# Retention followed by a two-layer dense block on one core: token order restored in the copy ahead of the dense product, stores of whole rows, casts of v behind the copies of k and q, and block 1 computed undivided

## The chip, the cores and the metric

The kernel runs on one core of a Trainium2 chip. A core has five engines that each work through their own list of instructions in order: TensorE (PE, matrix products; its weight loads are listed apart as PEld), VectorE (DVE), ScalarE (ACT), GpSimd (POOL) and SyncE (SP, which here only issues DMAs). Waiting is done on semaphores, and 16 DMA engines move data between the main memory and the core's SBUF. TensorE writes to PSUM, eight banks of 128 partitions by 512 fp32; VectorE and ScalarE read it. The metric is the device time of one execution in microseconds; lower is better.

## The reference

Four batches of eight heads, 768 tokens each, head width 64: for each head, a state of 64 x 64 decays by a factor gamma per token and takes in k v^T, and each token's output is q times the state. The eight heads of a token side by side make a row of 512, and 3072 such rows go through a dense block with a leaky activation:

```python
for t in range(S):
    state = gamma * state + k[t] v[t]^T          # per batch and head
    y[t]  = scale * q[t] state
x = y.transpose(0, 2, 1, 3).reshape(3072, 512)   # heads side by side
h = x @ w_in                                     # 512 x 2048
g = max(h, 0) + alpha * min(h, 0)
out = g @ w_out                                  # 2048 x 512, rows in token order
```

## The kernel before, in words

**Windows and blocks.** The recurrence is computed in chunks. A window `w` is 256 tokens of one batch and four heads (group g of two); there are 24. Four windows (512 tokens, both groups) make a block `n` of the dense part; there are six. A chunk c is half a window, 128 tokens. In SBUF a partition p holds the token pair 2p, 2p+1 (the loads at L141 read "h (p a) d -> p h (a d)"), so the tokens of a chunk are kept as a parity a and an index i: column 64a + i.

**A window's steps.** `load` (L135) issues three DMAs for k, q and v on SP. `prep` (L150) scales k and q into `kdq` (L158, on POOL or DVE) and casts v to fp16 into `vx` (L176 on ACT for windows 0 to 7, L178 on POOL later). k and q must be transposed into `kq`: windows 0 to 7 do it in `turn` (L189) with eight TensorE transposes into a PSUM tile `trb` and one ACT copy (L201); windows 8 to 23 do it with a transposing DMA that SP issues (L171). `scores` (L214) makes 16 small products into the PSUM tile `sc`; `state_sums` (L238) sums k v^T into `st`; `masked` (L254, DVE) applies the mask to `sc`; `state` (L265, DVE) updates the state `tg`; `within` (L299) makes the outputs `y` from the carried state (L286) and from the products within the chunk (L308), then sets a small DVE memset (L317) that tells they are through; `finish` (L321) adds the other carried products and copies `y` from PSUM to SBUF as fp16, `xT` (L329, ACT). `y` and `sc` have one buffer each, so `within` of a window waits for the copy of the window before it. `visit(old, new)` is the usual order: `within(old)`, `scores(new)`, `state_sums(new)`, `finish(old)`, `masked(new)`, `state(new)`.

**Token order before.** `xT` keeps the columns parity by parity, so the dense product's row 64a + i of 128 rows is token 2i + a, and the store (L435) puts them back on the way out: `out[row : row + 128, :].rearrange("(p a) m -> a p m", a=2)`.

**Dense part.** `ffn1` (L370) computes 16 tiles of 128 x 512, each with four matmuls (L377, moving operand `xT[n][:, hp, :]`, 512 columns); ACT takes relu of minus the tile (L367) and DVE combines (L356) into `gt`. `ffn2` (L412) has four groups of 16 matmuls (L422), each closed by an ACT copy (L431) and a store of 256 KB (L435). Both are generators that are advanced matmul by matmul with `tick(gen, m)`: the order is written out by hand, and each engine runs its instructions in that order. Block 1's first product runs as two halves of 256 columns (`ffn1_half`, L388, matmuls at L398), between which windows 6 and 7 are worked in (L540 to L564).

**The opening** (L446 to L514): windows 0 to 3 one after another, with filler matmuls (`busy`, L181) that write an unused tile. The weights come by eight DMAs issued on POOL (`get_wi`, `get_wo`); the loads of windows 4 to 11 wait for the third `get_wo`.

**The later blocks** (L566 on): `ahead` (L551) puts `prep(w)` and the loads of window w+4 in between; SP thus issues, in program order, transposing DMAs, loads and stores from one queue.

Of the kernel before, what the change touches and what calls it, by code (L numbers as in the profile page):

```python
# [10 lines left out]
F16 = mybir.dt.float16  # L11
# [7 lines left out]
def kernel(  # L19
# [15 lines left out]
    nc = tc.nc  # L35
# [7 lines left out]
    WB = 4  # L43
# [106 lines left out]
    def prep(w, opening=False, k_on=None):  # L150
        u, g, b, c3 = place(w)
        t = staged.pop(w)
        kdq = sbp.tile([128, 2, 4, 2, D], F16, tag="kdq", bufs=8, name=f"kdq{w}")
        vx = sbp.tile([128, 4, 2, D], F16, tag="vx", bufs=8, name=f"vx{w}")
        kq = sbp.tile([128, 8, 128], F16, tag="kq", bufs=8, name=f"kq{w}")

        def scaled(eng, kind, src):
            eng.tensor_tensor(  # L158
                out=kdq[:, kind].rearrange("p z r d -> p r z d"),
                in0=src.rearrange("p (r x) (a d) -> p r (x a) d", a=2, x=2),  # L160
                in1=tab[:, 16 * kind + 8 * g : 16 * kind + 8 * g + 8]
                .rearrange("p (r z) -> p r z", r=2)
                .unsqueeze(3)
                .to_broadcast([128, 2, 4, D]),
                op=MULT,
            )

        scaled(k_on or (nc.vector if opening else nc.gpsimd), 0, t["k"])
        scaled(nc.gpsimd, 1, t["q"])
        if w >= NPE:  # L170
            nc.sync.dma_start_transpose(  # L171
                out=kq, in_=kdq.rearrange("p k z r d -> p (k z r d)")
            )
        v_in = t["v"].rearrange("p h (a d) -> p h a d", a=2)
        if opening:
            nc.scalar.activation(out=vx, in_=v_in, func=COPY, bias=0.0, scale=1.0)  # L176
        else:
            nc.gpsimd.tensor_copy(out=vx, in_=v_in)  # L178
        prepped[w] = (kdq, kq, vx)

    def busy(m):  # L181

# [3 lines left out]
                out=ips[:, 0:128], lhsT=ones, rhs=ones, start=True, stop=True  # L186
            )

    def turn(w, tag, fill=0):  # L189
        kdq, kq, vx = prepped[w]  # L190
        flat = kdq.rearrange("p k z r d -> p (k z r d)")
        trb = ps("trb", tag, 1024, F16)
        for i in range(8):
            if i == 4 and fill:
                busy(fill)
            nc.tensor.transpose(  # L196
                out=trb[:, 128 * i : 128 * i + 128],
                in_=flat[:, 128 * i : 128 * i + 128],
                identity=ident,
            )  # L200
        nc.scalar.activation(  # L201
            out=kq.rearrange("p b i -> p (b i)"),
            in_=trb[:, 0:1024],
            func=COPY,
            bias=0.0,
            scale=1.0,
        )

    DIAG = [(0, 0), (1, 1), (0, 1), (1, 0)]

# [67 lines left out]
    def carried(w, y, started, same, after=None):  # L278
        u, g, b, c3 = place(w)
        kq = live[w][1]  # L280
        for x in range(2):
            for r in range(2):
                c = r if same else 1 - r
                if c3 + c == 0:
                    continue
                ins = nc.tensor.matmul(  # L286
                    out=y[half(x), 512 * c + 128 * r : 512 * c + 128 * r + 128],
                    lhsT=tgs[2 * u + c, g][half(r), x, :],
                    rhs=kq[half(r), 4 + 2 * x : 6 + 2 * x, half(c)],
                    start=(c, x) not in started,  # L290
                    stop=not same,
                    skip_group_check=True,
                )
                started.add((c, x))
                if after is not None:
                    behind(ins, after, "the other row half wrote this bank")
                    after = None

    def within(w):  # L299
        u, g, b, c3 = place(w)  # L300
        vx, m2 = live[w][2:4]
        y = ps("y", "y", 1024, FP, 1)
        started = set()
        carried(w, y, started, True)
        for r in range(2):
            for a in range(2):
                for c, x in DIAG:
                    last = nc.tensor.matmul(  # L308
                        out=y[half(x), 512 * c + 128 * r : 512 * c + 128 * r + 128],
                        lhsT=vx[half(c), 2 * r + x, a, :],  # L310
                        rhs=m2[half(c), 2 * r + x, a, :],
                        start=(c, x) not in started,
                        stop=(a == 1 and (c == r or c3 + c == 0)),
                        skip_group_check=True,
                    )
                    started.add((c, x))
        done = nc.vector.memset(warm[0:1], 0.0)  # L317
        behind(done, last, "tells that the products within the chunks are through")
        live[w].append((y, started, done))

    def finish(w):  # L321
# [3 lines left out]
        live.pop(w)  # L325
        n, i = divmod(u, 2)
        if w % WB == 0:
            xT[n] = sbp.tile([128, NP, TB], F16, tag="xT", bufs=2, name=f"xT{n}")
        nc.scalar.activation(  # L329
            out=xT[n][:, 2 * g : 2 * g + 2, TU * i : TU * i + TU].rearrange(  # L330
                "p r (c i) -> p c r i", c=2
            ),
            in_=y.rearrange("p (c z) -> p c z", c=2)[:, :, 0:256].rearrange(
                "p c (r i) -> p c r i", r=2
            ),
            func=COPY,
            bias=0.0,
            scale=1.0,
# [31 lines left out]
    def ffn1(n, order="spyfSpYf"):  # L370
# [3 lines left out]
        for ft in range(NFT):  # L374
            hps = banks.next("hps")
            for hp in range(NP):
                nc.tensor.matmul(  # L377
                    out=hps,
                    lhsT=w_in_all[:, hp, 128 * ft : 128 * ft + 128],
                    rhs=xT[n][:, hp, :],  # L380
                    start=(hp == 0),
                    stop=(hp == NP - 1),
                )
                if hp == NP - 1:
                    prelu(gt, ft, hps, 0, TB, minus(hps))
                yield

    def ffn1_half(n, i, order):  # L388
        if i == 0:
            gts[n] = sbp.tile([128, NFT, TB], F16, tag="gt", bufs=2, name=f"gt{n}")  # L390
        gt = gts[n]
        lo, hi = TU * i, TU * i + TU
        banks = Banks(order)
        for f0 in range(0, NFT, 2):
            hps = banks.next("hps")
            for j in range(2):
                for hp in range(NP):
                    nc.tensor.matmul(  # L398
                        out=hps[:, TU * j : TU * j + TU],
                        lhsT=w_in_all[:, hp, 128 * (f0 + j) : 128 * (f0 + j) + 128],  # L400
                        rhs=xT[n][:, hp, lo:hi],
                        start=(hp == 0),
                        stop=(hp == NP - 1),
                    )
                    if j == 1 and hp == NP - 1:
                        hm = minus(hps)
                        for z in range(2):
                            s = slice(TU * z, TU * z + TU)
                            prelu(gt, f0 + z, hps[:, s], lo, hi, hm[:, s])
                    yield  # L410

    def ffn2(n, parts=1, order="f"):  # L412
        gt = gts.pop(n)
# [3 lines left out]
        for f0 in range(0, NFT, step):  # L417
            for tq in range(4):
                if f0 == 0:
                    opss[tq] = banks.next("ops")  # L420
                for ft in range(f0, f0 + step):
# [7 lines left out]
                    if ft == NFT - 1:  # L429
# [2 lines left out]
                            out=os_sb, in_=opss[tq], func=COPY, bias=0.0, scale=1.0  # L432
                        )
                        row = TB * n + 128 * tq
                        nc.sync.dma_start(  # L435
                            out=out[row : row + 128, :].rearrange("(p a) m -> a p m", a=2),
                            in_=os_sb,
                        )
                    yield

    def tick(gen, m):
# [32 lines left out]
    aps = ps("aps", "f")  # L474
    nc.tensor.transpose(out=aps[:, 0:NFT], in_=alpha_sb, identity=tab[0:NFT, ALT : ALT + NFT])
    prep(2, opening=True)
    get_wi(0)
    state(0)
    nc.vector.tensor_scalar(
        out=oma_sb, in0=aps[:, 0:NFT], scalar1=-1.0, scalar2=1.0, op0=MULT, op1=ADD  # L480
    )
    turn(1, "f")
    within(0)
    scores(1)
    state_sums(1)
    finish(0)
    masked(1)
    prep(3, opening=True, k_on=nc.gpsimd)
    state(1)
    turn(2, "f")  # L490
    within(1)
    scores(2)
    state_sums(2, (0,))
    finish(1)
    masked(2)
    state(2, (0,))
    turn(3, "f")
    within(2)
    scores(3)
    state_sums(3, (0,))  # L500
    finish(2)
    masked(3)
    state(3, (0,))
    for i in range(1, 4):
        get_wi(i)
    get_wo(0)
    get_wo(1)
    held.append(get_wo(2))
    get_wo(3)
    within(3)  # L510
    busy(8)
    finish(3)
    for w in range(WB, 3 * WB):
        load(w)  # L514

    gen = ffn1(0)
    tick(gen, 32)
    for w in (2, 3):
        state_sums(w, (1,))
        state(w, (1,))  # L520
    for _ in gen:
        pass
    gen = ffn2(0)
    for w in range(WB, 2 * WB):
        prep(w, opening=True)
    tick(gen, 30)
    turn(4, "p")
    tick(gen, 6)
    visit(None, 4)
    tick(gen, 7)  # L530
    turn(5, "p")
    tick(gen, 6)
    visit(4, 5)
    tick(gen, 7)
    turn(6, "p")
    tick(gen, 6)
    visit(5, 6)
    for _ in gen:
        pass
    gen = ffn1_half(1, 0, "ffpp")  # L540
    tick(gen, 8)
    turn(7, "f")
    tick(gen, 8)
    visit(6, 7)
    tick(gen, 16)
    visit(7, None)
    for _ in gen:
        pass
    more = [8]

    def ahead():  # L551
# [4 lines left out]
                load(w + WB)  # L556
            more[0] += 1

    gen = ffn1_half(1, 1, "spyfSpYf")
    for i in range(WB):  # L560
        tick(gen, 14)
        ahead()
    for _ in gen:
        pass  # L564

    for n in range(1, NBLK):  # L566
        if n > 1:
            gen = ffn1(n)
            for i in range(2):
                tick(gen, 20)  # L570
                ahead()
            for _ in gen:
                pass
        gen = ffn2(n)
        if n + 1 < NBLK:
            w0 = WB * (n + 1)
# [46 lines left out]
```

## Time and profile before

| what | value |
|---|---|
| median of three runs | 246.69 us (243.04 to 247.25) |
| the profiled execution's own time | 245.44 us |
| its span, first to last instruction | 243.6 us |
| around the span | 1.84 us |
| PE busy | 212.6 us, 87% of the span |
| DVE, ACT, POOL busy | 130.5, 99.3, 58.4 us |
| granted TensorE clock, mean | 0.925 of full |
| moved by DMA | 34.08 MB |

A profile is read from its stages: for each stretch of the span, which engine is busy throughout, and where TensorE stands idle, what it waited for. A window of the trace gives the busy time of each engine in that stretch, the granted clock, the mean share of the 16 DMA engines that was busy, and GB/s. Shares over 1 occur, since a packet's time is counted where it ends. A matmul's listed duration contains its pipeline's length; the chain of work that ended last shows the spacing instead.

### The profile page before, as it was taken

The numbers are of one execution on the slowest core, as the hardware profiler recorded it, in microseconds if no ns is written. First come the engines' busy times: TensorE is split into PE (matmuls) and PEld (weight loads), VectorE is DVE, ScalarE is ACT, GpSimd is POOL, SyncE is SP. The second block draws the span as 40 slices with busy tenths as digits, with TensorE's granted clock in tenths as the row PEclk, the third lists the DMA queues.
The fourth block names the chain that finished last, engine by engine and source line by source line (L and its number), as shares of the span: only waits on it lengthen the run. The fifth ranks groups of instructions, "written<-read, shape, count | busy, mean of one in ns | idle before, by whom it ended". The sixth has DMA issues, their size and how long they took to land.

```text
span 243.6 us, 5296 instructions
## 1 busy us (share of the span) xinstructions
PE 212.6 (87%) x2215; PEld 112.3 (46%) x2215; DVE 130.5 (54%) x242; ACT 99.3 (41%) x162; POOL 58.4 (24%) x69
## 2 busy tenths in 40 slices
PE   8557999999489999999989999599999999999500
PEld 8445444456358654444444445244445444444200
DVE  1535288635639964288644786142887526840000
ACT  2353366454436423465114663024663126631100
POOL 1591002596000654410243501262000000000000
PEclk9955599999979999999999999979999999999955
DMA  7999998993195999695999699695993111001110
GB/s 209 317 169 205 201 211 256 311 340 109 51 71 136 237 230 153 176 74 167 96 257 110 178 71 197 130 263 70 71 86 94 42 47 51 37 0 32 51 51 38
DMA packets 62599, 34.08 MB, mean 140 GB/s; under 512 B 18400, under 2 KB 59504, under 8 KB 62576
## 3 DMA queue, kind: packets, MB, share of 16 engines
q1 hardware_dynamic: 58032, 29.37, 67.4%
q0 software_dynamic: 4224, 4.19, 10.7%
q8 instruction: 17, 0.28, 0.5%
q10 hardware_dynamic: 320, 0.19, 0.3%
q14 instruction: 6, 0.05, 0.1%
HBM read 27.45 MB, written 6.29 MB: 138 GB/s over the span
## 4 chain that ended last, share of the span: by engine, by line
PE 57%; DMA 18%; SPq 9%; ACT 3%; DVE 3%; POOL 2%; issue 2%; POOLq 0%; ACTq 0%
PE ops L422 25%; PE hps L377 18%; PE hps L398 7%; DMA vs<-in_v_dram 6%; DMA kq<-kdq 6%; SPq L171 5%; DMA ks<-in_k_dram 5%; SPq L141 4%; PE sc L222 2%; POOL kdq L158 2%; PE y L286 2%; DMA qs<-in_q_dram 1%; PE y L308 1%; DVE m L257 1%; ACT kq L201 1%
## 5 line engine op out<-in xcount | busy, mean ns | idle before, releaser
L356 DVE SCALAR_TENSOR_TENSOR gt<-hm,oma,hps 128x512 f16<-128x512 f32 (+1 forms) x112 | 73.7, 670 | 33.9 <-ACT hm L367 25.6
L422 PE MATMUL ops<-wout,gt 128*128 128x512 f16 x384 | 90.7, 385 | 0.0
L377 PE MATMUL hps<-xT,win 128*128 128x512 f16 x320 | 72.3, 387 | 0.3 <-DVE ss L272 0.3
L367 ACT ACTIVATE hm<-hps 128x512 f32<-128x512 f32 x96 | 57.3, 597 | 32.5 <-PE hps L377 24.4
L422 PEld LDWEIGHTS <-gt 128*128 128x128 f16 x384 | 35.6, 99 | 41.1 <-issue 2.4
L377 PEld LDWEIGHTS <-win 128*128 128x128 f16 x320 | 31.7, 100 | 39.4 <-issue 3.3
L257 DVE TENSOR_TENSOR m<-sc,mi 128x1024 f16<-128x1024 f32 x24 | 29.4, 1223 | 15.1 <-PE sc L222 13.5
L329 ACT ACTIVATE xT<-y 128x512 f16<-128x512 f32 x24 | 14.3, 597 | 50.8 <-PE y L286 49.8
L158 POOL TENSOR_TENSOR kdq<-qs,tab 128x512 f16<-128x512 f32 x24 | 25.7, 1070 | 33.6 <-DMA qs<-in_q_dram 33.6
L158 POOL TENSOR_TENSOR kdq<-ks,tab 128x512 f16<-128x512 f32 x17 | 17.8, 1049 | 56.6 <-PE hps L398 21.1
L431 ACT ACTIVATE os<-ops 128x512 f32<-128x512 f32 x24 | 14.3, 596 | 29.7 <-PE ops L422 29.6
L398 PE MATMUL hps<-xT,win 128*128 128x256 f16 x128 | 16.0, 285 | 2.2 <-ACT kq L201 1.2
L222 PE MATMUL sc<-kq 64*64 64x128 f16 x384 | 10.5, 230 | 7.7 <-ACT kq L201 4.4
L286 PE MATMUL y<-kq,tg 64*64 64x128 f16 x160 | 13.1, 248 | 4.4 <-DVE warm L317 1.9
L317 DVE MEMSET warm<- 1x1 f32 x24 | 1.4, 59 | 27.6 <-PE y L308 27.5
L398 PEld LDWEIGHTS <-win 128*128 128x128 f16 x128 | 12.8, 102 | 4.8 <-issue 2.5
L178 POOL CAST vx<-vs 128x512 f16<-128x512 f32 x16 | 9.9, 618 | 20.9 <-DMA vs<-in_v_dram 16.0
L286 PEld LDWEIGHTS <-tg 64*64 64x64 f16 x160 | 5.9, 108 | 16.2 <-issue 7.8
L275 DVE TENSOR_TENSOR tg<-ss,tab 128x128 f16<-128x128 f32 x32 | 12.1, 379 | 1.1
L222 PEld LDWEIGHTS <-kq 64*64 64x64 f16 x384 | 7.0, 112 | 10.9 <-ACT kq L201 5.4
L308 PE MATMUL y<-m,vx 64*64 64x128 f16 x384 | 11.2, 233 | 0.0
L201 ACT ACTIVATE kq<-trb 128x1024 f16<-128x1024 f16 x8 | 8.1, 1018 | 4.7 <-PE trb L196 4.7
(24 smaller groups left out, 77.1 us busy)
## 6 DMA issues: line engine op xcount, KB each, us to landing
ks<-in_k_dram SPq DMA_DIRECT2D x24, 256.0 KB
qs<-in_q_dram SPq DMA_DIRECT2D x24, 256.0 KB
vs<-in_v_dram SPq DMA_DIRECT2D x24, 256.0 KB
out_dram<-os SPq DMA_DIRECT2D x24, 256.0 KB
win<-in_moe_w_in_dram POOLq DMA_DIRECT2D x4, 512.0 KB, 6.5
wout<-in_moe_w_out_dram POOLq DMA_DIRECT2D x4, 512.0 KB, 14.6
kq<-kdq SPq DMA_TRANSPOSE x16
mi<-mi_const ACTq DMA_DIRECT2D x1, 128.0 KB
```

The costliest lines, as they stand in the source:

```text
L158: eng.tensor_tensor(out=kdq[:, kind].rearrange("p z r d -> p r z d"), in0=src.rearrange("p (r x) (a d) -> p r (x a) d", a=2, x=2), in1=tab ...
L222: nc.tensor.matmul(out=sc[half(c), at : at + 128], lhsT=kq[half(r), 2 * x + a, half(c)], rhs=kq[half(r), 4 + 2 * x : 6 + 2 * x, half(c)], ...
L257: nc.vector.tensor_tensor(out=m2.rearrange("p s a i -> p s (a i)"), in0=sc.rearrange("p (s n) -> p s n", n=256), in1=mask.unsqueeze(1).to_ ...
L286: ins = nc.tensor.matmul(out=y[half(x), 512 * c + 128 * r : 512 * c + 128 * r + 128], lhsT=tgs[2 * u + c, g][half(r), x, :], rhs=kq[half(r ...
L308: last = nc.tensor.matmul(out=y[half(x), 512 * c + 128 * r : 512 * c + 128 * r + 128], lhsT=vx[half(c), 2 * r + x, a, :], rhs=m2[half(c), ...
L329: nc.scalar.activation(out=xT[n][:, 2 * g : 2 * g + 2, TU * i : TU * i + TU].rearrange("p r (c i) -> p c r i", c=2), in_=y.rearrange("p (c ...
L356: nc.vector.scalar_tensor_tensor(out=gt[:, ft, lo:hi], in0=hm, scalar=oma_sb[:, ft : ft + 1], in1=hps, op0=MULT, op1=ADD,)
L367: nc.scalar.activation(out=hm, in_=hps, func=RELU, bias=0.0, scale=-1.0)
L377: nc.tensor.matmul(out=hps, lhsT=w_in_all[:, hp, 128 * ft : 128 * ft + 128], rhs=xT[n][:, hp, :], start=(hp == 0), stop=(hp == NP - 1),)
L398: nc.tensor.matmul(out=hps[:, TU * j : TU * j + TU], lhsT=w_in_all[:, hp, 128 * (f0 + j) : 128 * (f0 + j) + 128], rhs=xT[n][:, hp, lo:hi], ...
L422: nc.tensor.matmul(out=opss[tq], lhsT=gt[:, ft, 128 * tq : 128 * tq + 128], rhs=w_out_all[:, ft, :], start=(ft == 0), stop=(ft == NFT - 1),)
L431: nc.scalar.activation(out=os_sb, in_=opss[tq], func=COPY, bias=0.0, scale=1.0)
```

## The change

1. The copy in `finish` reads `y` with a step (parity innermost, two elements 64 apart) and writes `xT` in natural token order. `xT` becomes `[128, 2, 4, 2, 128]` (group, chunk, head pair, token), and `ffn1` reads `xT[n][:, hp // 2, :, hp % 2, :]`: four runs of 128 columns, 256 apart. `y` uses columns 256 to 767 of its two banks, one unbroken stretch.
2. The store is `out[row : row + 128, :]`, one partition per row.
3. The casts of v of windows 0 to 7 move out of `prep` into `turn`: behind the copy of k and q, or ahead of it with `v_first` (windows 4 to 7).
4. `within` makes its carried products last.
5. Opening: the weights' DMAs are issued after `prep(3)`, `turn(w+1)` stands between the scores of w and `finish(w-1)`, and eight filler matmuls stand ahead of each of windows 1 to 3 and around the last `finish`.
6. Block 1 uses `ffn1` whole; windows 6 and 7 are worked in during block 0's `ffn2`.

```diff
-            nc.scalar.activation(out=vx, in_=v_in, func=COPY, bias=0.0, scale=1.0)
+            v_ins[w] = v_in
...
+    def cast_v(w):
+        nc.scalar.activation(
+            out=prepped[w][2], in_=v_ins.pop(w), func=COPY, bias=0.0, scale=1.0
+        )
-    def turn(w, tag, fill=0):
+    def turn(w, tag, fill=0, v_first=False):
...
+        if v_first:
+            cast_v(w)
         nc.scalar.activation(
             out=kq.rearrange("p b i -> p (b i)"),
...
+        if not v_first:
+            cast_v(w)
...
-                    out=y[half(x), 512 * c + 128 * r : 512 * c + 128 * r + 128],
+                    out=y[half(x), 256 + 256 * c + 128 * r : 384 + 256 * c + 128 * r],
...
-            xT[n] = sbp.tile([128, NP, TB], F16, tag="xT", bufs=2, name=f"xT{n}")
+            xT[n] = sbp.tile([128, 2, 4, 2, 128], F16, tag="xT", bufs=2, name=f"xT{n}")
         nc.scalar.activation(
-            out=xT[n][:, 2 * g : 2 * g + 2, TU * i : TU * i + TU].rearrange(
-                "p r (c i) -> p c r i", c=2
-            ),
-            in_=y.rearrange("p (c z) -> p c z", c=2)[:, :, 0:256].rearrange(
-                "p c (r i) -> p c r i", r=2
-            ),
+            out=xT[n][:, g, 2 * i : 2 * i + 2].rearrange("p c r (i a) -> p (c r) i a", a=2),
+            in_=y[:, 256:768].rearrange("p (s a i) -> p s i a", a=2, i=64),
...
-                    rhs=xT[n][:, hp, :],
+                    rhs=xT[n][:, hp // 2, :, hp % 2, :],
...
-                        nc.sync.dma_start(
-                            out=out[row : row + 128, :].rearrange("(p a) m -> a p m", a=2),
-                            in_=os_sb,
-                        )
+                        nc.sync.dma_start(out=out[row : row + 128, :], in_=os_sb)
...
-    get_wi(0)
...
     prep(3, opening=True, k_on=nc.gpsimd)
-    state(1)
-    turn(2, "f")
-    within(1)
-    scores(2)
...
+    for i in range(4):
         get_wi(i)
...
+    for w in range(1, WB):
+        busy(8)
+        scores(w)
+        state_sums(w, (0,) if w > 1 else None)
+        if w + 1 < WB:
+            turn(w + 1, "f")
+        finish(w - 1)
+        masked(w)
+        state(w, (0,) if w > 1 else None)
+        within(w)
     busy(8)
     finish(3)
+    busy(8)
...
     tick(gen, 30)
-    turn(4, "p")
-    tick(gen, 6)
+    turn(4, "p", v_first=True)
+    tick(gen, 5)
     visit(None, 4)
-    tick(gen, 7)
-    turn(5, "p")
+    tick(gen, 8)
+    turn(5, "p", v_first=True)
     tick(gen, 6)
     visit(4, 5)
-    tick(gen, 7)
-    turn(6, "p")
-    tick(gen, 6)
+    tick(gen, 1)
+    turn(6, "p", v_first=True)
+    tick(gen, 5)
     visit(5, 6)
+    turn(7, "p", v_first=True)
+    tick(gen, 5)
+    visit(6, 7)
     for _ in gen:
         pass
-    gen = ffn1_half(1, 0, "ffpp")
...
     visit(7, None)
...
-    gen = ffn1_half(1, 1, "spyfSpYf")
...
     for n in range(1, NBLK):
-        if n > 1:
-            gen = ffn1(n)
...
+        gen = ffn1(n)
+        for i in range(4 if n == 1 else 2):
+            tick(gen, 14 if n == 1 else 20)
+            ahead()
```

More of the change, by code (lines that the diff above doesn't have):

```diff
@@ L179, in prep @@
         prepped[w] = (kdq, kq, vx)
+    v_ins = {}
     def busy(m):
@@ L290, in carried @@
                     start=(c, x) not in started,
-                    stop=not same,
+                    stop=(same == (c == r)),
                     skip_group_check=True,
@@ L297, in carried @@
                     after = None
+        return ins
     def within(w):
@@ L303, in within @@
         started = set()
-        carried(w, y, started, True)
         for r in range(2):
@@ L307, in within @@
                 for c, x in DIAG:
-                    last = nc.tensor.matmul(
-                        out=y[half(x), 512 * c + 128 * r : 512 * c + 128 * r + 128],
+                    nc.tensor.matmul(
+                        out=y[half(x), 256 + 256 * c + 128 * r : 384 + 256 * c + 128 * r],
                         lhsT=vx[half(c), 2 * r + x, a, :],
@@ L312, in within @@
                         start=(c, x) not in started,
-                        stop=(a == 1 and (c == r or c3 + c == 0)),
+                        stop=(a == 1 and c3 + c == 0),
                         skip_group_check=True,
@@ L316, in within @@
                     started.add((c, x))
+        last = carried(w, y, started, True)
         done = nc.vector.memset(warm[0:1], 0.0)
@@ L386, in ffn1 @@
                 yield
[L388 to L403, printed above, removed]
-                    )
[L405 to L410, printed above, removed]
     def ffn2(n, parts=1, order="f"):
@@ L434, in ffn2 @@
                         row = TB * n + 128 * tq
-                        nc.sync.dma_start(
-                            out=out[row : row + 128, :].rearrange("(p a) m -> a p m", a=2),
-                            in_=os_sb,
-                        )
+                        nc.sync.dma_start(out=out[row : row + 128, :], in_=os_sb)
                     yield
@@ L483 @@
     within(0)
[L484 to L487, printed above, removed]
     prep(3, opening=True, k_on=nc.gpsimd)
-    state(1)
-    turn(2, "f")
-    within(1)
-    scores(2)
[L493 to L504, printed above, removed]
+    for i in range(4):
         get_wi(i)
@@ L509 @@
     get_wo(3)
-    within(3)
+    for w in range(1, WB):
[8 more added lines that the diff above has]
+        within(w)
     busy(8)
     finish(3)
+    busy(8)
     for w in range(WB, 3 * WB):
         load(w)
-    gen = ffn1(0)
-    tick(gen, 32)
+    for _ in ffn1(0):
+        pass
     for w in (2, 3):
@@ L520 @@
         state(w, (1,))
-    for _ in gen:
-        pass
     gen = ffn2(0)
@@ L526 @@
     tick(gen, 30)
-    turn(4, "p")
-    tick(gen, 6)
+    turn(4, "p", v_first=True)
+    tick(gen, 5)
     visit(None, 4)
-    tick(gen, 7)
-    turn(5, "p")
+    tick(gen, 8)
+    turn(5, "p", v_first=True)
     tick(gen, 6)
     visit(4, 5)
-    tick(gen, 7)
-    turn(6, "p")
-    tick(gen, 6)
+    tick(gen, 1)
+    turn(6, "p", v_first=True)
+    tick(gen, 5)
     visit(5, 6)
+    turn(7, "p", v_first=True)
+    tick(gen, 5)
+    visit(6, 7)
     for _ in gen:
         pass
-    gen = ffn1_half(1, 0, "ffpp")
[L541 to L545, printed above, removed]
     visit(7, None)
-    for _ in gen:
-        pass
     more = [8]
@@ L557, in ahead @@
             more[0] += 1
-    gen = ffn1_half(1, 1, "spyfSpYf")
[L560 to L564, printed above, removed]
-    for n in range(1, NBLK):
-        if n > 1:
-            gen = ffn1(n)
[L569 to L573, printed above, removed]
+    for n in range(1, NBLK):
+        gen = ffn1(n)
+        for i in range(4 if n == 1 else 2):
+            tick(gen, 14 if n == 1 else 20)
+            ahead()
+        for _ in gen:
+            pass
         gen = ffn2(n)
```

## The prediction

> **What bounds the kernel now.** I read the page's slices first, then the windows by stage, then the waits.
>
> ```profile
> PE   8557999999489999999989999599999999999500
> PEclk9955599999979999999999999979999999999955
> DMA  7999998993195999695999699695993111001110
> ```
>
> TensorE is busy in almost every slice, so it is the bound, except in four places: slices 2 to 4 (clock at half), 10 to 11, 25 to 26, and the last two, where no engine computes and the DMA engines are at a tenth.
>
> ```profile
> 59.88:71.40 11.52, 7.42 (x113) 5.26 (x111) 6.72 (x18) 4.54 (x8) 0.00 (x0) 0.85 0.92 63
> 100.20:133.00 32.80, 32.12 (x346) 15.20 (x344) 21.75 (x38) 14.23 (x24) 10.21 (x12) 1.00 1.09 153
> 133.00:169.30 36.30, 33.70 (x330) 15.59 (x328) 19.97 (x34) 14.22 (x24) 10.78 (x13) 0.95 0.99 151
> 169.30:201.14 31.84, 31.84 (x337) 15.22 (x336) 20.10 (x36) 14.26 (x24) 0.45 (x1) 1.00 0.60 68
> ```
>
> (Columns: stretch, length, busy PE, PEld, DVE, ACT, POOL, granted clock, DMA share, GB/s.) The stretch 169.30 to 201.14 is one block with its four visits at full clock and no gap: 31.84 us. The two alike before it took 32.80 and 36.30. That is 0.96 + 4.46 = 5.4 us of loss, in which TensorE waits for the transposing DMAs or runs cold behind such a wait.
>
> **The tail and the stores.**
>
> ```profile
> 219.07 10.87 SPq L435 DMA_DIRECT2D out_dram<-os  x4
> 228.81 0.60 ACT L431 ACTIVATE os<-ops 128x512 f32<-128x512 f32 x1 [2.86 <-PE ops L422]
> 220.00:221.00 1.00, 1.00 0.10 20
> 241.00:242.00 1.00, 0.50 0.13 49
> 242.00:243.00 1.00, 0.50 0.01 4
> 0.74 0.47 SPq L141 DMA_DIRECT2D ks<-in_k_dram  x1
> 3.79 0.69 DVE L158 TENSOR_TENSOR kdq<-ks,tab 128x512 f16<-128x512 f32 x1 [2.78 <-DMA ks<-in_k_dram]
> 7.00:8.00 1.00, 1.00 1.15 346
> 108.00:110.00 2.00, 1.00 0.13 51
> PE sc L222 <- DMA kq<-kdq: 3.3, 3, 2.6
> 111.01 10.38 DMA vs<-in_v_dram
> ```
>
> In the window rows the last three numbers are clock, DMA share and GB/s; the other rows begin with start and length in us, and the waits' row gives total, times and longest. While only stores move, the share is 0.13, two engines of sixteen (2/16 = 0.125), at 51 GB/s. The old store's outermost step has two values, the parity. The loads, whose outermost step is 128 partitions, reach share 1.15 and 346 GB/s. The last four stores (1.05 MB) start at 220.2 (0.10/0.125 of that microsecond is busy) and end near 242.1: 5.5 us each. The last is issued near 229.4 and waits for its forerunners, so the program ends 14.2 us after the last copy (243.6 - 229.4). The row at 108 to 110 shows the same earlier: fourteen engines idle, two finishing stores, and a load of v issued at 111.01 that takes 10.38 us; its packets lie on all sixteen, two of them behind the stores.
>
> **The change, part by part.**
>
> *Stores as whole rows (-10.6 us tail, -5.4 us middle).* The new outermost step is 128 on both sides, as in the loads, so I take sixteen engines: 5.5/8 = 0.7 us a store, 0.76 by 262 KB at 346 GB/s. After the last copy come 0.04 us to the issue, 1.1 to the first byte (219.07 to 220.2), 0.7 moving and 1.5 from the last byte to the end (242.1 to 243.6): 3.4. The slower bound is a load in the opening: 3.05 us from issue to use (0.74 to 3.79) and 0.8 to close, 3.9. I take 3.6, so 14.2 - 3.6 = 10.6. In the middle each block's four stores held two engines for 4 x 5.5 = 22 of 32 us, now 3. The stalls of 5.4 us (the row of 3.3 us of waits, the rest cold clock behind the longest) then have no cause left; bounds 0 and 5.4, and I take 5.4, since in the two stalled blocks the late loads sit behind those stores.
>
> *Block 1 undivided, windows 6 and 7 worked in earlier (-4.2 us).*
>
> ```profile
> 47.49 0.63 ACT L176 ACTIVATE vx<-vs 128x512 f16<-128x512 f32 x1 [1.67 <-DMA vs<-in_v_dram]
> 56.76 0.45 PE trb L196 x8
> 58.90 0.22 PE sc L222 x16
> 66.12 0.29 DVE tg L275
> 71.47 10.66 PE hps L398 x96
> 201.14 13.81 PE hps L377 x64
> L257 DVE TENSOR_TENSOR m<-sc,mi 128x1024 f16<-128x1024 f32 x24 | 29.4, 1223 | 15.1 <-PE sc L222 13.5
> ```
>
> The half product runs from 59.88 to 82.12 (71.47 + 10.66), 22.24 us. Half matmuls run at 10.66/96 = 111 ns, so 128 of them are 14.2, against 13.81 for 64 whole ones. With eight transposes (0.45) and two visits (some 0.85 and 0.35 of short products, the scores 0.22 of them) the work is 15.9; 6.4 are gaps, where TensorE waits for relu, the kq copy, and two combines, mask and state in DVE's queue (the stage's first 11.52 us hold only 7.42 busy). After the change these waits mostly lie beside `ffn2`'s matmuls (216 ns each). What is left, by durations: the transposes of window 7 reuse a bank that `state(6)` frees, mask 1.23 + 0.28 behind scores with only 0.2 of products in between: 1.35. Before `visit(7, None)` four matmuls (0.86) cover most of a mask, 0.2 left; then its memset queues behind `state(7)` (three operations of some 0.29), 0.5; then the xT copy against two matmuls, 0.25. With hand-overs 2.5 against 6.4 and 0.4 for the halves: 4.3, taken as 4.2. The casts of v ahead of the kq copies cost nothing, ACT being free there while the transposes run; were v late, scores would wait with it, but v of window 7 is cast at 47.5 in the trace and needed near 57.
>
> *Opening (-2.4 us).*
>
> ```profile
> 9.52 0.40 PE L196 MATMUL trb<-mi,kdq 128*128 128x128 f16 x4 [0.40 <-POOL kdq L158]
> 10.66 0.63 ACT L176 ACTIVATE vx<-vs 128x512 f16<-128x512 f32 x1 [2.62 <-DMA vs<-in_v_dram]
> 13.15 0.63 ACT L176 ACTIVATE vx<-vs 128x512 f16<-128x512 f32 x1 [1.86 <-DMA vs<-in_v_dram]
> 13.69 1.01 ACT L201 ACTIVATE kq<-trb 128x1024 f16<-128x1024 f16 x1
> 14.75 0.64 PE sc L222 x8
> 16.34 0.52 ACT vx L176
> 16.86 0.92 ACT kq L201
> 21.07 0.47 PE sc L222 x13
> 25.33 9.07 PE hps L377 x32
> 8.97:12.38 3.41, 1.02 (x25) 1.00 1.00 291
> 26.03:29.44 3.41, 3.41 (x9) 0.50 1.24 206
> 60.15:63.57 3.42, 2.27 (x30) 1.00 0.14 53
> 63.57:66.98 3.41, 1.46 (x57) 1.00 0.13 49
> 24.00:25.00 1.00, 0.50 1.23 202
> 33.55 0.37 SPq L141 DMA_DIRECT2D ks<-in_k_dram  x1
> ```
>
> Window 1's kq copy stands behind two casts that wait for v, though its transposes end at 9.92. Without them it runs 9.95 to 10.96, and `scores(1)` starts at 11.2, not 14.75. But the change adds a wait. ACT now does kq (0.92), v (0.52) and only then xT of the window before, and `within` needs the one `y` buffer that xT frees. A turn is then within 0.35, filler 0.5, scores and sums 0.45, transposes 0.45, ACT 2.05, hand-overs 0.2: 4.0 us warm, against 3.1 before (scores of windows 1 and 3 at 14.75 and 20.9, two turns apart). So `scores(3)` comes at 19.3, `ffn1(0)` at 22.9 if the clock stays full, against 25.3.
>
> The clock decides. Its changes fit a grid of 3.41 us: the rows show a window with 1.46 us busy (43%) followed by half clock (the clock of 59.88 to 71.40 is 0.85), one with 1.02 (30%) likewise, one with 2.27 (66%) followed by full clock, and a full one that brings it back. The new turns are 1.95 of 4.05 us busy; the worst window has 41%. I take a fall near 15.8: half clock stretches the last two turns, `ffn1(0)` starts at 25.5, and the denser window from 22.6 to 26.0 brings the full clock at 26.0 instead of 29.44. Its end moves from 42.26 to 39.8: 2.4. Bounds: always full, 37.0 (5.3); cold for one window more, 42.4 (0).
>
> The Trainium skill ("TensorE: Matmul & The Clock Gate", "Why this matters for your kernels") asks only for no idle gap over about 3 us. By that the new opening, whose gaps are 2 us, stays warm; the trace disagrees, as 63.57 to 66.98 is idle for under 2 us in all and fell.
>
> The weights: `get_wi(0)` passes window 3's k and q on POOL, so its start moves from 11.2 to 13.4; the seven others hardly move. They come at 202 GB/s (4.19 MB, 20.7 us), all by about 35.5, before `ffn2(0)` needs them; the loads held behind the third `get_wo` go from 33.55 to some 35, and window 7, whose v is then cast near 49, is needed near 57: that slack covers it, and without it each late microsecond is one of `ffn2(0)`.
>
> *The copy into natural order (0, bound +2.1).* It reads pairs 256 bytes apart; no row shows that. Below, 597 ns as now. Above, each element at half rate, which adds what another 512 elements add to the kq copy (1018 - 597 = 0.42); it is on the path at xT of windows 0 to 3 and 7: 2.1. I take 0, the nearest row being this copy itself, which already steps from run to run of 128 at 597 ns. The Trainium skill ("SBUF — State Buffer", "Door 1: The DMA port swizzle") says that PSUM has lines of 8 bytes and that other patterns slow matmuls; it speaks against this read, and the sum by it would be the upper bound. No run here shows it.
>
> *Memory steps of the product's moving operand (0).* Four runs of 128 columns in place of 512. The scores' operand already has runs of 64, and their sixteen products of 128 columns, four side by side, take 0.22 us: the spacing of unbroken columns (512 in 0.216).
>
> **The sum.** 245.44 - 10.6 - 5.4 - 4.2 - 2.4 = 222.8, forecast **223 us**. The profiled execution lies 1.25 under the median and 2.4 above the lowest run, which goes into the range.
>
> **The rivals.**
> *The opening stays warm:* 223 - 2.9 = 220. The fillers speak for it, the 43% row against.
> *The transfers are slow by themselves:* if loads and transposing DMAs, not stores, set the middle, TensorE runs into the same waits at the same times, the gains before them are lost, and the tail alone remains: 245.44 - 10.6 = 235. Against: fourteen idle engines in the row at 108 to 110.
> *The stores aren't spread* (the change doesn't do what it says): 239, or 245 if the waits also eat the early gains. Loads with the same outermost step are spread.
> *Slower:* the moving operand's jumps slow `ffn1`. Its place is 384 matmuls; each has 216 ns, and above (245.4 - 222.8)/384 = 59 ns more, 275 ns, the kernel loses. At half rate it would be 223 + 83 = 306. Against: the scores' runs.
>
> **How the numbers follow.** Forecast 0.70, warm 0.15, slow transfers 0.07, unspread 0.04, slower 0.04. Low end: warm opening, then the lowest run's 2.4 and a little of block 1's gaps, 217. High end: opening +2.4, copy +2.1, one cold window in block 1 (+1.7, half of 3.41), the median's +1.25: 231. A change within 2% (4.9 us) is about what the runs' own spread (4.2 us) hides. Faster: 0.70 + 0.15 + 0.07 + half of unspread = 0.94; same 0.02; slower 0.04.
>
> **What would show it.** Right: the last store ends within 4 us of the last copy; DMA share never long at 0.13; no wait of L222 for transposing DMAs; blocks 2 to 4 at 31.8 us each; block 0's end of `ffn1` near 40 and block 1's near 75. Wrong: a matmul spacing of `ffn1` above 216 ns, an xT copy of 1 us, a half clock past 30, or stages 100 to 169 still longer than 31.84.

## The result and the profile after

The changed kernel takes **224.37 us** (median of four, 222.90 to 225.69) against 245.96 us for the kernel before, measured beside it: a ratio of **0.9157**, 95% interval 0.9031 to 0.9282. In a second series, with more runs, it was 225.19 us, a ratio of 0.9207 (0.9160 to 0.9253). Ratios and their intervals are taken from the fast runs alone, so a ratio isn't always that of the two medians. The forecast was 223 us. The profiled execution took 225.53 us with a span of 223.8 us, 19.8 us under the span of before.

The slices of the page after, 40 over the span:

```profile
PE   8666899999789999999999999999999999999993
PEclk9995589999999999999999999999999999999999
DMA  6959999999549969399427599031450012100112
```

Counted from 0, two of the four weak places of before are gone: slices 25 to 26 (the middle) and the two empty ones at the end. Slices 10 to 11 (block 1) are better, 7 and 8 tenths busy where they were 4 and 8. One place is as it was: slices 3 and 4 still have the half clock.

The windows by stage after (columns as in the prediction):

```profile
42.26:64.50 22.24, 20.24 (x298) 11.00 (x299) 13.54 (x28) 10.60 (x17) 14.13 (x15) 1.00 0.80 245
96.81:128.62 31.81, 31.81 (x345) 15.18 (x344) 20.68 (x38) 14.23 (x24) 10.59 (x12) 1.00 0.68 165
128.62:160.44 31.82, 31.82 (x330) 15.14 (x328) 19.53 (x34) 14.23 (x24) 7.80 (x9) 1.00 0.55 141
160.44:192.28 31.84, 31.84 (x337) 15.19 (x336) 20.11 (x36) 14.26 (x24) 0.00 (x0) 1.00 0.17 51
```

The three blocks that took 32.80, 36.30 and 31.84 us now take 31.81, 31.82 and 31.84, and TensorE is busy for all of each. In the trace after no scores wait for a transposing DMA any more.

The end after, in the timeline (first two rows) and in the windows (the last numbers are clock, DMA share, GB/s):

```profile
217.11 3.79 SPq L419 DMA_DIRECT2D out_dram<-os  x2
219.94 0.60 ACT L415 ACTIVATE os<-ops 128x512 f32<-128x512 f32 x1 [2.85 <-PE ops L406]
221.00:222.00 1.00, 1.00 0.61 240
```

The last copy ends at 220.54; the last store moves in the microsecond from 221, at a share of 0.61 where it was 0.13, and the span ends 3.3 us after the copy (14.2 before). The page of the profile gives 2.3 us from issue to landing for a store.

Put side by side, span against span, before and after:

| stage | before, us | after, us | moved | forecast |
|---|---|---|---|---|
| to the end of `ffn1(0)` | 42.26 | 42.26 | 0.0 | -2.4 |
| `ffn2(0)` and block 1's `ffn1` | 39.86 | 36.27 | -3.6 | -4.2 |
| from there to the last copy's start | 146.69 | 141.41 | -5.3 | -5.4 |
| last copy's start to the end | 14.8 | 3.9 | -10.9 | -10.6 |
| span | 243.6 | 223.8 | -19.8 | -22.6 |

### The profile page after: what moved, and what is told of

Same layout as the page of the kernel before. It is cut to its first block, busy times and chain, and to the rows that moved or that the text cites. A ratio compares the mean times of both kernels' runs of the same rounds, so it can differ in the third digit from the quotient of the medians.

```text
span 223.8 us, 5215 instructions
## 1 busy us (share of the span) xinstructions
PE 210.0 (94%) x2183; PEld 107.1 (48%) x2183; DVE 128.7 (58%) x226; ACT 99.0 (44%) x162; POOL 58.2 (26%) x69
## 3 DMA queue, kind: packets, MB, share of 16 engines
q0 software_dynamic: 4224, 4.19, 11.5%
## 4 chain that ended last, share of the span: by engine, by line
PE 89%; DVE 5%; ACT 3%; issue 0%; DVEq 0%
PE hps L385 38%; PE ops L406 36%; PE idle L187 4%; PE y L319 4%; PE sc L233 3%; DVE m L268 3%; PE trb L203 2%; PE y L297 2%; ACT kq L210 1%; PE st L257 1%; DVE tg L286 1%; ACT xT L341 1%; DVE kdq L158 1%; ACT vx L192 0%; DVE ss L283 0%
## 5 line engine op out<-in xcount | busy, mean ns | idle before, releaser
L364 DVE SCALAR_TENSOR_TENSOR gt<-hm,oma,hps 128x512 f16<-128x512 f32 x96 | 71.7, 747 | 32.1 <-ACT hm L375 21.7
L406 PE MATMUL ops<-wout,gt 128*128 128x512 f16 x384 | 89.2, 380 | 0.0
L385 PE MATMUL hps<-xT,win 128*128 128x512 f16 x384 | 85.8, 385 | 0.2 <-ACT xT L341 0.2
L385 PEld LDWEIGHTS <-win 128*128 128x128 f16 x384 | 37.9, 99 | 46.6 <-issue 2.6
L319 PE MATMUL y<-m,vx 64*64 64x128 f16 x384 | 10.5, 229 | 5.2 <-ACT xT L341 3.8
L297 PE MATMUL y<-kq,tg 64*64 64x128 f16 x160 | 12.0, 237 | 1.8 <-DVE tg L286 1.2
L319 PEld LDWEIGHTS <-vx 64*64 64x64 f16 x384 | 6.8, 110 | 14.1 <-issue 11.0
L187 PE MATMUL idle<-ones 128*128 128x128 f16 x102 | 10.4, 278 | 1.1 <-DVE warm L433 1.1
L283 DVE TENSOR_TENSOR ss<-tg,st 128x128 f32<-128x128 f16 x32 | 9.0, 282 | 1.5
L187 PEld LDWEIGHTS <-ones 128*128 128x128 f16 x102 | 8.8, 129 | 1.6 <-DVE warm L433 1.1
```

The lines of the kernel that those rows point to most:

```text
L187: nc.tensor.matmul(out=ips[:, 0:128], lhsT=ones, rhs=ones, start=True, stop=True)
L297: ins = nc.tensor.matmul(out=y[half(x), 256 + 256 * c + 128 * r : 384 + 256 * c + 128 * r], lhsT=tgs[2 * u + c, g][half(r), x, :], rhs=kq[ ...
L319: nc.tensor.matmul(out=y[half(x), 256 + 256 * c + 128 * r : 384 + 256 * c + 128 * r], lhsT=vx[half(c), 2 * r + x, a, :], rhs=m2[half(c), 2 ...
L364: nc.vector.scalar_tensor_tensor(out=gt[:, ft, lo:hi], in0=hm, scalar=oma_sb[:, ft : ft + 1], in1=hps, op0=MULT, op1=ADD,)
L385: nc.tensor.matmul(out=hps, lhsT=w_in_all[:, hp, 128 * ft : 128 * ft + 128], rhs=xT[n][:, hp // 2, :, hp % 2, :], start=(hp == 0), stop=(h ...
L406: nc.tensor.matmul(out=opss[tq], lhsT=gt[:, ft, 128 * tq : 128 * tq + 128], rhs=w_out_all[:, ft, :], start=(ft == 0), stop=(ft == NFT - 1),)
```

## The experiments

Two questions were open: whether the number of DMA engines that share a store explains both the tail and the middle, or token order and whole rows have a part; and why the opening gained nothing. The theory for the opening was the clock (filler matmuls, and how densely TensorE works), its rival ScalarE's queue, in which the change puts xT behind the kq copy and the cast of v. The cuts of code below show what is changed, not the whole edit where it is long.

### Old order, store cut in two by parity

```diff
-nc.sync.dma_start(out=out[row : row + 128, :].rearrange("(p a) m -> a p m", a=2), in_=os_sb)
+pairs = out[row : row + 128, :].rearrange("(p a) m -> a p m", a=2)
+for a in range(2):
+    nc.sync.dma_start(out=pairs[a], in_=os_sb[64 * a : 64 * a + 64, :])
```

> The kernel before, with each store cut into two by parity (64 partitions to every second row); token order in SBUF, opening and block 1 stay as they were. If what counts is over how many DMA engines a store spreads, its outermost step is now 64 and the tail and the middle come down as in the changed kernel: 246 - 10.9 - 5.3, about 230 us, and no DMA share held at 0.13. If the restored order or the contiguous rows are what counts, nothing moves: 246 us, or a little more for 24 further issues on SP.

Measured: 229.94 us (227.56 to 230.66), ratio 0.9394 (0.9330 to 0.9459). The chain of this run shows the starts of `ffn1` in blocks 2 to 4 (31.8 us apart), and the windows its last store:

```profile
100.60 13.81 PE hps L377 x64
132.41 13.81 PE hps L377 x64
164.22 13.81 PE hps L377 x64
```

```profile
225.00:226.00 1.00, 1.00 0.53 121
226.00:227.00 1.00, 1.00 0.60 141
```

Token order is still undone by the store, and every second row still skipped. What changed is that each store is two DMAs, and that the outermost step of each has 64 values in place of 2. That removes the middle's waits (no scores wait for a transposing DMA in this trace) and most of the tail (4.1 us after the last copy), about 15 of the 21 us. Two DMAs on two engines each would be a share of 0.25; the rows show 0.53 and 0.60. So the spread of the store over the DMA engines is the cause, and natural order is one way to get it.

### The changed kernel with the old store

```diff
-nc.sync.dma_start(out=out[row : row + 128, :], in_=os_sb)
+nc.sync.dma_start(out=out[row : row + 128, :].rearrange("(p a) m -> a p m", a=2), in_=os_sb)
```

The copy in `finish` keeps the parity order here.

> The changed kernel with the old store and the parity order in the copy; opening, casts and block 1 as changed. If the tail and the middle hang on the store alone and the gain of block 1 survives a middle with waits: 224.4 + 10.9 + 5.3, about 240.5 us. If the middle's waits have fixed times, as with slow transfers, the earlier gain is waited away: about 244 to 246 us.

Measured: 245.57 us (241.89 to 251.35), ratio 0.9990 (0.9936 to 1.0045): no gain is left, neither block 1's nor any other, within the interval. First, from the timeline of this run, TensorE's waits for a transposing DMA:

```profile
122.83 0.58 PE L233 MATMUL sc<-kq 64*64 64x128 f16 x16 [2.69 <-DMA kq<-kdq]
158.57 0.42 PE L233 MATMUL sc<-kq 64*64 64x128 f16 x16 [2.12 <-DMA kq<-kdq]
```

And the same in the kernel before:

```profile
122.67 0.42 PE L222 MATMUL sc<-kq 64*64 64x128 f16 x16 [0.26 <-DMA kq<-kdq]
157.85 0.42 PE L222 MATMUL sc<-kq 64*64 64x128 f16 x16 [2.60 <-DMA kq<-kdq]
```

In this profiled execution, of 246.22 us, block 1's `ffn1` ended at 79.9 instead of 82.1, but window 14's scores start at 122.8 in both, and window 18's at 158: the transfers arrive at the same clock time, and TensorE waits 2.69 us where it waited 0.26. With the old store the middle is set by the transfers, and time gained ahead of it is waited away. The parts of the change don't add up one by one: the store is worth 15 to 16 us alone, the rest some 5 us with it (229.94 to 224.37 or, in the second series, 225.19) and nothing that shows without it.

### Block 1 in halves again

```diff
-gen = ffn1(n)                       # n = 1, after visit(7, None)
+gen = ffn1_half(1, 0, "ffpp")       # turn(7), visit(6, 7), visit(7, None) in between
+gen = ffn1_half(1, 1, "spyfSpYf")
```

> The changed kernel with block 1 as before: ffn1 in two halves, windows 6 and 7 worked in between them. By the profiles the undivided block was worth 36.3 against 39.85 us, so 224.4 + 3.6 = 228 us. If the transfers or the clock give the gain back somewhere later: 224 to 225 us.

Measured: 228.79 us (227.78 to 229.62), ratio 0.9386 (0.9345 to 0.9427): 4.4 us over the changed kernel's first series, 3.6 over its second. By the profiles 2.5 us of that lie in this stage, 38.79 us here against 36.27; the opening, whose code is the same in both, also ended 0.6 us later in this execution. The timeline of this run, the four waits inside the half product:

```profile
63.23 1.05 PE L406 MATMUL hps<-xT,win 128*128 128x256 f16 x8 [1.15 <-DVE gt L364]
65.90 0.24 PE L297 MATMUL y<-kq,tg 64*64 64x128 f16 x2 [0.87 <-DVE warm L329]
67.21 1.91 PE L406 MATMUL hps<-xT,win 128*128 128x256 f16 x16 [1.07 <-DVE tg L286]
70.79 0.24 PE L297 MATMUL y<-kq,tg 64*64 64x128 f16 x2 [1.27 <-DVE warm L329]
```

They are gaps of the kind that the prediction listed, 4.4 us of them. That this equals the difference of the medians is chance, for the changed kernel keeps some 2.1 us of gaps:

```profile
59.43 0.61 PE L203 MATMUL trb<-mi,kdq 128*128 128x128 f16 x8 [1.34 <-DVE tg L286]
63.07 0.42 PE L319 MATMUL y<-m,vx 64*64 64x128 f16 x16 [0.16 <-DVE m L268]
64.01 0.24 PE L297 MATMUL y<-kq,tg 64*64 64x128 f16 x2 [0.47 <-DVE warm L329]
64.95 13.54 PE L385 MATMUL hps<-xT,win 128*128 128x512 f16 x62 [0.15 <-ACT xT L341]
```

Transposes of window 7 behind the bank of `state(6)`, 1.34 (forecast 1.35); the mask 0.16 (0.2); the memset behind `state(7)` 0.47 (0.5); the xT copy 0.15 (0.25). The stage took 39.86 us before and 38.79 here, halves in both: before, TensorE ran 3.4 us of it at half clock (0.85 of full from 59.88 to 71.40), here none.

### Fillers in the opening's gap

```diff
         state(w, (0,) if w > 1 else None)
+        busy(24 if w < 3 else 10)
         within(w)
```

> The changed kernel with 24, 24 and 10 more filler matmuls in the opening, ahead of within(1), within(2) and within(3), where TensorE stands idle for the y buffer or the mask. If the clock is what kept the opening from gaining: no window falls under 43% busy, the clock stays full, ffn1(0) starts near 23 and ends near 37 instead of 42.26, and the time is about 219.5 us. If ScalarE's queue alone sets the opening: 224 us, or up to 2 more for fillers that outlast the gap.

Measured: 223.09 us (221.14 to 223.62), ratio 0.9116 (0.9061 to 0.9172), whose interval overlaps the changed kernel's. From this run's chain and its windows (last numbers: clock, DMA share, GB/s):

```profile
14.17 2.67 PE idle L187 x24
25.98 13.81 PE hps L385 x64
14.00:17.00 3.00, 3.00 (x36) 0.50 0.54 65
17.00:20.00 3.00, 3.00 (x75) 0.93 1.25 206
```

The clock had already fallen near 11, so the first fillers took 2.67 us; a window without a gap brought the full clock back near 17, and `ffn1(0)` ran at 216 ns throughout (13.81 us against 15.53 in the changed kernel). Yet it started at 25.98, only 0.4 us earlier. So the half clock is worth about 1.7 us of `ffn1(0)`, and something else holds its start; the fillers are no free test of that, since the first 24 outlast the gap that they fill.

### xT ahead of the kq copy (e4)

```diff
-        if w + 1 < WB:
-            turn(w + 1, "f")
         finish(w - 1)
+        if w + 1 < WB:
+            turn(w + 1, "f")
         masked(w)
```

> The changed kernel with finish(w-1) ahead of turn(w+1) in the opening, so that ScalarE frees y before it copies kq and casts v. If the added wait for y is what lengthens a turn: some 1 to 1.5 us off each of two turns, 221.5 to 222.5 us at the same clock, and under 220 if the denser turns also keep the clock full. If the clock alone counts and still falls: 224 us.

> The changed kernel itself, beside e4 on one chip, so that the two can be compared directly: 224 us.

> e4 (xT ahead of the kq copy in the opening) beside the changed kernel on one chip. If the place of xT is worth what the profiles show (ffn1(0) starts at 20.4 instead of 26.4, part of it given back where the loads behind the weights come late): 219.5 to 220.5 us, 4 us under the changed kernel. If the first comparison was the chips' difference: 224 us.

Measured: 220.11 us (218.87 to 222.44), ratio 0.9041 (0.8969 to 0.9112). On one chip with the changed kernel: 220.35 us, ratio 0.9021 (0.8976 to 0.9065), against 225.19 us, 0.9207 (0.9160 to 0.9253): the intervals are apart, and this order is 4.8 us better than the changed kernel. The changed kernel's chain in the opening:

```profile
12.85 1.02 ACT kq L210
13.88 0.52 ACT vx L192
14.40 0.50 ACT xT L341
...
26.36 15.53 PE hps L385 x64
```

And this experiment's timeline, ScalarE and the start of `ffn1(0)`:

```profile
11.77 0.60 ACT L341 ACTIVATE xT<-y 128x512 f16<-128x512 f32 x1 [0.77 <-PE y L297]
12.27 1.02 ACT L210 ACTIVATE kq<-trb 128x1024 f16<-128x1024 f16 x1
20.42 13.98 PE L385 MATMUL hps<-xT,win 128*128 128x512 f16 x64
```

In the changed kernel `within(1)` waits through kq, v and xT; here xT runs first and `within` starts earlier. The scores of windows 1 and 2, one turn apart and all at full clock, give the price; first the changed kernel, then this one:

```profile
11.72 0.42 PE L233 MATMUL sc<-kq 64*64 64x128 f16 x16
15.89 0.54 PE L233 MATMUL sc<-kq 64*64 64x128 f16 x16
```

```profile
11.07 0.42 PE L233 MATMUL sc<-kq 64*64 64x128 f16 x16
13.78 0.42 PE L233 MATMUL sc<-kq 64*64 64x128 f16 x16
```

A turn takes 4.17 us with xT behind kq and v, 2.71 with xT first (the next one 3.00). Over two turns that is some 2.6 us. `ffn1(0)` starts at 20.42 instead of 26.36, but this is the fastest of the executions, and its clock never fell; the changed kernel ran at half clock from 16.0 on. So the 5.9 us hold the clock too.

### Two more orders, and how much of it is the clock

```diff
# e7: the order of the opening before, casts of v behind the kq copies
# e9: xT first as above, and without the fillers
-        busy(8)        # in each of the three turns, and on both sides of finish(3)
```

> The changed kernel with the order of the opening as before, only the casts of v behind the kq copies: kq of window 1 is early, and xT stands ahead of the next kq copy. If the gain of the casts was eaten by the new place of xT: scores(1) near 11.5 and two turns of 3 us, ffn1(0) from about 21 to 22, and 220 to 222 us. If the filler matmuls and the new order carried what the opening has: 224 us or more, with a half clock up to 29.

> e4 without the filler matmuls of the three turns and around the last finish (40 of them). If the fillers keep the clock: it falls within the opening, as at 43% busy before, and the time is 222 to 225 us. If the clock holds without them, 0.55 us a turn go, but the loads behind the weights take that over: 219.5 to 220 us.

Measured: the old order 220.90 us, ratio 0.9050 (0.9001 to 0.9098); without fillers 221.01 us, 0.9087 (0.9045 to 0.9129). The old order's chain row and window first, then those of the run without fillers:

```profile
20.78 14.43 PE hps L385 x64
14.00:17.00 3.00, 2.68 (x62) 0.50 1.20 194
```

```profile
21.15 15.31 PE hps L385 x64
14.00:17.00 3.00, 2.96 (x64) 0.50 0.61 77
```

Both ran at half clock from 11.5 or 13.7 on and still started `ffn1(0)` near 21, more than 5 us ahead of the changed kernel. The run without fillers fits neither of its forecasts: the clock fell, and the time stayed within 1 us of that with fillers. But both also leave out fillers, which take 4.0 us of the changed kernel's chain in the opening (0.55 a set of eight at full clock, 0.97 at half), so these two don't part the place of xT from the fillers. What does is the last experiment below, whose opening is that of e4, fillers and all, and whose clock was at half for 6.3 us ahead of `ffn1(0)`:

```profile
23.65 14.13 PE hps L385 x64
```

One opening, xT first, thus starts `ffn1(0)` at 20.42, 21.84 (e4's second series) or 23.65 us, with the half clock ahead of it for 0, 3.4 and 6.3 us. With xT behind kq and v, and half clock for some 10 us, it is 26.36, and 26.55 in the second series (27.41 and 28.11 in the two experiments above that keep this opening). So the latest start with xT first is 2.7 us ahead of the earliest with xT behind. The starts with xT first spread over 3.2 us; 1.2 of them are there already at `scores(1)` (11.07 against 12.26), and the rest goes with the half clock and the fillers that it slows. The clock adds 0.6 to 1.7 us in `ffn1(0)` itself (14.43, 15.31 and 15.53 against 13.81). The old order with the casts of v moved starts `ffn1(0)` at 20.78 where the kernel before did at 25.33: casting v behind the copy of kq gives its gain where xT isn't put behind both.

### More fillers, and matmuls ahead of the last transposes

```diff
# e5, on e4
+        busy(10)          # ahead of each within
# e10, on e4
-    tick(gen, 30)
+    tick(gen, 25)
...
     visit(5, 6)
+    tick(gen, 5)
     turn(7, "p", v_first=True)
```

> The opening of e4 (xT ahead of the kq copy) with ten more filler matmuls ahead of each within, in the gap of 0.6 to 1.15 us behind the mask. If e4's spread (218.9 to 222.4 us) comes from windows in which the clock falls: a smaller spread and about 219 us. If e4 is already held by the loads that wait for the weights: 220 us as e4.

> e4 with five of ffn2(0)'s matmuls moved from ahead of turn(4) to ahead of turn(7), where TensorE waits 1.34 us for the bank that state(6) frees. If that wait is on the path: 1.1 us fewer, about 219 us. If windows 4 to 7, now five matmuls earlier, run into the loads that wait for the weights: 220 us or slower.

Measured: 221.69 us, ratio 0.9085 (0.9041 to 0.9130), and 220.68 us, 0.9023 (0.8986 to 0.9059). Neither is a gain over e4, and both miss the 219 us that was hoped for; the fillers' spread (220.04 to 222.24) is that of e4's second series (219.24 to 221.49). A row of e10's timeline, VectorE's first mask of block 1, and then rows of the chain of e4's second series, the last of them the same mask:

```profile
47.73 1.22 DVE L268 TENSOR_TENSOR m<-sc,mi 128x1024 f16<-128x1024 f32 x1
```

```profile
18.19 17.64 DMA wout<-in_moe_w_out_dram
...
42.37 4.46 DMA ks<-in_k_dram
...
47.55 1.13 DVE m L268
```

In both, this mask of window 4 stands in VectorE's queue behind k of window 7, which VectorE waits 1.6 us to land, and that load is one of those held behind the third `get_wo`. Although `ffn2(0)` starts at 38.1 in one and 36.1 in the other, the masks run at nearly the same times. The move did what it was for, as the wait ahead of the transposes of window 7 shrank from 1.35 to 0.16 us, but from this mask to the end of block 1's `ffn1` both take 25.7 us. And the chain that ended last in e4 runs through the weights' DMA, the loads' issues on SP and this load, not through TensorE's opening. So in these executions e4 is held by the loads behind the weights; moving them wasn't tried.

## Why the prediction was right, and where it was not

**The forecast held**, 223 against 224.37 us, and three of the four terms were right in mechanism and within 0.6 us in size. The median flatters it: the sum was made from a profiled execution, and profile against profile it is 222.8 against 225.53 us, 2.8 us short, 2.4 of them the opening.

- *Tail:* 10.6 forecast, 10.9 measured; 3.3 us after the copy, just under the lower of the two bounds (3.4). Confirmed by the cut store, which has a short tail, 4.1 us, in the old order.
- *Middle:* 5.4 forecast, 5.3 measured, with the blocks at 31.8 us and no wait for transposing DMAs. The rival of slow transfers is refuted by the cut store. The prediction was right to hold 239 and 245 us open for a store that isn't spread: with the old store the early gains are waited away, 245.57.
- *Block 1:* 4.2 forecast, 3.6 in the profiles, of which its own undoing shows 2.5 in the stage; each remaining gap is within 0.1 us of its term. What was read too simply is the stage before: its 6.4 us "are gaps, where TensorE waits", but TensorE was idle for 4.1 us of it (7.42 busy in 11.52) and ran 3.4 us at half clock. With the halves put back the clock stayed full, so the part of the gain that was clock isn't in the 2.5.
- *Copy and moving operand:* both 0, as taken. The page's row after:

```profile
L341 ACT ACTIVATE xT<-y 128x512 f16<-128x512 f32 x24 | 14.3, 597 | 43.4 <-PE y L297 40.7
```

  The copy with pairs 256 bytes apart takes 597 ns as before, and a matmul of `ffn1` 216 ns (13.81 us for 64, in the chain rows above). The Trainium skill ("SBUF — State Buffer", "Door 1: The DMA port swizzle") gives PSUM lines of 8 bytes and warns of non-contiguous patterns for matmuls; a ScalarE read of that kind shows no price here.

- *Opening:* **wrong in size**, 2.4 forecast, 0.0 measured, on the bound given. Two steps failed. The smaller is "the denser window from 22.6 to 26.0 brings the full clock at 26.0". In the run after the clock fell at 16.0 and came back at 29.7, four windows of 3.41 us. On that grid:

```profile
12.61:16.02 3.41, 1.47 (x40) 1.00 0.38 53
22.85:26.26 3.41, 2.92 (x41) 0.50 1.24 206
26.26:29.67 3.41, 3.41 (x10) 0.50 1.22 196
```

  The fall after 43% busy came as forecast (half clock from 16.0). But 2.92 of 3.41 us busy, 86%, did not bring the clock back; only the full window to 29.67 did, 3.4 us later than forecast, which is 1.7 us of `ffn1(0)`. The Trainium skill ("TensorE: Matmul & The Clock Gate", "Why this matters for your kernels") warns of idle gaps over about 3 us; this trace doesn't agree, as the longest gap in the window that fell was 1.94 us. The other step is the start, "`ffn1(0)` starts at 25.5": it was 26.36, 0.9 later, and `scores(1)` came at 11.72 where 11.2 was forecast. The added wait was seen and rightly priced at full clock (4.0 us a turn, measured 4.17). But the 3.1 us of before that it was set against are turns at half clock, and at half clock the new turn took 5.47 us (15.89 to 21.36). The wait, and the half clock that it helps to bring on, eat what the earlier kq copy gives: undoing it gained 4.8 us of time. Of the signs given, block 0's `ffn1` ended at 42.3, not near 40, and block 1's at 78.5, not near 75; the others of being right came. That the predicted total still came out within 1.4 us rests on the other terms and on the median.

## What to carry to other kernels

Look at the DMA share while only one kind of transfer moves: here a share held at 2 of 16 was a store whose outermost step had two values, and it delayed the loads and transposing DMAs queued with it, not only its own bytes. Gains ahead of a stage that transfers pace can be waited away there, so remove the pacing first and measure the parts together. Before moving an instruction up in an engine's queue, ask which single buffer is freed by what it now stands in front of.

## What the runs showed that was not expected

The prediction's rule for the clock, by the busy share of a window of 3.41 us, isn't borne out. Two windows of one execution, e4's second series, on the grid of its clock's changes:

```profile
7.65:11.06 3.41, 2.21 (x59) 1.00 1.11 331
17.89:21.30 3.41, 2.20 (x67) 1.00 1.24 205
```

Both are 64 to 65% busy at full clock; the half clock followed the first and the full clock the second. In the old order of the opening even a window of 80% (8.13 to 11.54, idle for 0.66 us in all) was followed by half clock, and in the changed kernel one of 60% (9.20 to 12.61) by full clock. On the way back, windows at half clock with 86% (above) to 92% (13.70 to 17.11 without fillers) stayed there, and one with 89% (18.37 to 21.78 in the old order) came back. What the clock goes by is left open; with xT first, one opening started `ffn1(0)` anywhere from 20.42 to 23.65 us.

Fillers are no safe means either: at half clock 24 of them took 2.67 us where the gap to fill was 1.9, and 40 of them more or less (220.35 against 221.01 us, in different series) is within what these runs can tell.
